# Forgetting attention and a channel mix on one core: the instruction scheduler starts from seeded due times and keeps another pass

## The chip, the cores and the metric

The kernel runs on one core of one Trainium2 chip. The metric is the device time of one execution, in microseconds (us). The core has five engines with queues of their own: PE (TensorE, with PEld for its weight loads), DVE (VectorE), ACT (ScalarE), POOL (GpSimd) and SP (SyncE), which here only issues DMAs.

## What is computed

The reference is an attention with a forgetting bias, and a channel mix on its output. Cut to what matters:

```python
B, H, S, D = 8, 8, 576, 64             # channel mix: d_model 512, d_ff 1024, all float32
scores = (q @ k.T) / sqrt(D)           # per batch and head
cum = cumsum(maximum(s, 0))
scores = where(causal, -1e9, scores + minimum(-(cum[:, None] - cum[None, :]), 0))
attn = exp(scores - scores.max(-1)); attn = attn / (attn.sum(-1) + 1e-9)
x = (attn @ v)                         # heads side by side: (B, S, 512)
x_prev = x shifted by one token
xk = mu_k * x + (1 - mu_k) * x_prev
xr = mu_r * x + (1 - mu_r) * x_prev
out = sigmoid(xr @ w_r) * (maximum(xk @ w_k, 0) ** 2 @ w_v)
```

## The kernel before

**Tiling.** Attention is worked in visits: one visit is a pair of heads of one batch. Batches 0 and 1 are made in an older form (`scores`, line 1226 on, matmuls on lines 1247, 1258 and 1269, PE transposes on line 1649, sums on line 1770); batch 0 is cut into the first three query tiles (A, 64 + 128 + 128 queries) for all four pairs of heads, and then the other two (Z). Batches 2 to 7 are 24 visits of `split_scores`: per head six products, each of two accumulating matmuls on line 1344 (KH with G, then KL with QL, 67 rows), then DVE (line 1356, mask and minimum), ACT (line 1371, exponential), ACT and DVE (lines 1380 and 1387, the reciprocal), ACT (line 1396) and DVE (line 1402), which write the weights as two float16 halves. The DMA turns them, and `sum_values` multiplies them with V for both heads: 32 matmuls in a row on line 1530, into one PSUM tile named pair. `mix_pair` (line 1558 on) mixes neighbouring tokens and splits the result into halves for the channel mix (xkh, xkl on lines 1617 and 1620, by POOL, ACT or DVE).

**The channel mix** takes chunks of 256 tokens, 18 in all. Per chunk there are 96 matmuls of 256 columns with w_k (line 2019), ACT's relu (line 2033) and squares, 24 of 512 columns with w_r (line 2096), ACT's tanh (line 2110), and 48 of 512 columns with w_v (line 2150), whose product DVE takes (line 2161) and a DMA stores. A chunk can be worked as soon as the pairs of heads that cover its tokens are done. The inputs of chunk 0 come straight from the A visits: ACT on line 1947 and DVE on line 1963 mix them. The weights are loaded in a 64-bit form and split into halves by POOL (lines 894, 902), ACT (909, 932, 947) and DVE (914, 921, 938, 960) while the first visits run.

**PSUM.** Scores use two banks named s and two named t, the channel mix two named m, the pair tile the remaining two.

**What sets the order.** Nothing is issued as it is written. Class `Plan` (line 55 on) records each operation as a task: engine, planned length, the tasks that it depends on, and a due time that the program sets by hand (`plan.due`). Helpers `pe`, `act`, `dve`, `pool`, `dma` work out the planned length from columns and a constant (`over` for PE, `extra` for the others); `or_act`, `or_dve`, `or_pool` give a task a second engine that may take it. `Plan.forward` (line 141) is a list scheduler: it runs a model of the engines in time and, whenever one is free, takes the ready task with the least due time. `Plan.backward` (line 295) goes back from the end and returns new due times. `Plan.run` (line 347) repeats forward and backward 60 times and issues the order of the pass whose modelled end was earliest. While PE's first regular scores have not been reached, the scheduler also fills gaps of PE with a matmul of 192 columns on the identity, whose result nobody reads (`one_idle`, its matmul on line 494).

Of the kernel before, what the change touches and what calls it, by code (L numbers as in the profile page):

```python
# [54 lines left out]
class Plan:  # L55
# [283 lines left out]
        return [-x for x in at]  # L339


    PASSES = 60
    engines = ('DVE', 'ACT', 'POOL', 'SP', 'PE')
    LATER = 300.0
    LOCK = 1.0

    def run(self):
        best = None
        due = [t[4] for t in self.tasks]
        for _ in range(self.PASSES):  # L350
            found = self.forward(due)
            if best is None or found[2] < best[2]:
                best = found
            due = self.backward(found[1], found[4])
        order, _, _, emits, on = best
        for n, i in enumerate(order):
            for emit in emits.get(n, ()):
                emit()
            (self.tasks[i] if on[i] == self.tasks[i][0] else self.others[i])[2]()
# [3 lines left out]
def forgetting_attention_then_channel_mix(  # L363
# [16 lines left out]
    nc = tc.nc  # L380

    B, H, D, S = q.shape
    DM, DF = moe_w_k.shape
# [4 lines left out]
    CT = 256  # L388
# [49 lines left out]
    def pool(emit, reads, writes, n, extra, rate=0.8333, quarters=(0, 0)):  # L438
        return at_quarters(plan.add("POOL", n * rate + extra, emit, reads, writes), quarters)
# [895 lines left out]
    def split_scores(passes, F):  # L1335
# [5 lines left out]
        def products(ps, q, m, k0, n):  # L1341
            for x, (G, K, r) in enumerate(passes):
                pe(
                    lambda x=x, G=G, K=K, r=r: nc.tensor.matmul(  # L1344
                        ps.get()[:m, :n],
                        G.get()[:r, q : q + m],
                        K.get()[:r, k0 : k0 + n],
                        start=x == 0,
                        stop=x == 1,
                    ),  # L1350
                    [(G, x) for x in range(2)] + [(K, x) for x in range(2)], [ps], n, m,
                )

        def least(ps, n, mask, i):
# [203 lines left out]
    def mix_pair(b, c, found):  # L1558
# [8 lines left out]
        xm = late_space["xm"]  # L1567
# [13 lines left out]
        for w in range(2):  # L1581
            t = late_space[f"t{w}"]

            def mixed(w=w, t=t):
                nc.vector.scalar_tensor_tensor(
                    out=xm.get()[:, 0:S] if w == 0 else values(), in0=values(),
                    scalar=mu_late.ap[:, w, 0, c : c + 1], in1=t.get()[:, 0:S],
                    op0=ALU.mult, op1=ALU.add,
                )

            dve(
                mixed, [t, (t, "z"), (mu_late, w)] + ([found] if w == 0 else []),
                [found if w else xm], S, extra=100,
            )
        t0 = S * b
        at = t0 % RING
# [3 lines left out]
        for w in range(2):  # L1600
            src = xm if w == 0 else found

            def whole(o, n, w=w):
                return xm.get()[:, o : o + n] if w == 0 else found.get()[:, 448 + o : 448 + o + n]

            for o, n in pieces:
                some = range((t0 + o) // CT, (t0 + o + n - 1) // CT + 1)

                def own(y, o=o, n=n, w=w):
                    p = (t0 + o) % RING  # L1610
                    return row(w, y, c, p, p + n)

                his = [(chunk(w, 0, x), (c, b)) for x in some]
                los = [(chunk(w, 1, x), (c, b)) for x in some]

                def high(engine, own=own, whole=whole, o=o, n=n):
                    engine.tensor_copy(own(0), whole(o, n))  # L1617

                def low(engine, own=own, whole=whole, o=o, n=n):
                    engine.tensor_tensor(out=own(1), in0=whole(o, n), in1=own(0), op=ALU.subtract)  # L1620

                def high_act(own=own, whole=whole, o=o, n=n):
                    nc.scalar.copy(own(0), whole(o, n))

                if w == 0:
                    or_act(
                        pool(lambda f=high: f(nc.gpsimd), [src], his, n, 150),
                        high_act, n, 75,
                    )
                    or_dve(  # L1630
                        pool(lambda f=low: f(nc.gpsimd), [src] + his, los, n, 210, 2.0),
                        lambda f=low: f(nc.vector), n, both=True,
                    )
                else:
                    act(high_act, [src], his, n, 75)
                    dve(lambda f=low: f(nc.vector), [src] + his, los, n)
# [260 lines left out]
    def channel_mix(ch, start, span, after):  # L1897
# [111 lines left out]
        def hidden(fp):  # L2009
# [34 lines left out]
            if ch in range(6):  # L2044
                act(
                    lambda: nc.scalar.activation(kh.get()[:, fs, :], r.get(), AF.Square, scale=2.0**-6),
                    [r], [(kh, fp)], 2 * CT, 75,
                )
                y = act(
                    lambda: nc.scalar.activation(r.get(), r.get(), AF.Square),  # L2050
                    [], [r], 2 * CT, 75,
                )
                or_dve(
                    y,
# [14 lines left out]
            def sq():  # L2069
# [1 line left out]

            act(
                lambda: nc.scalar.activation(kh.get()[:, fs, :], r.get(), AF.Square, scale=2.0**-6),
                [r], [(kh, fp)], 2 * CT, 75,
            )
            dve(
                lambda: nc.vector.scalar_tensor_tensor(
# [12 lines left out]
        def gate(tt):  # L2090
# [32 lines left out]
            def scaled(engine):  # L2123
# [6 lines left out]
                pool(  # L2130
                    lambda: scaled(nc.gpsimd), scale_keys(sc, 3), [(g, 0), (g, DM // 2)], DM, 300
                ),
                DM, 94,
            )
            st["g", tt] = g

# [324 lines left out]
```

## Time and profile before

| | |
|---|---|
| median of 3 runs | 766.78 us (765.98 to 767.72) |
| the profiled execution | 766.97 us, of which its span, first to last instruction, is 765.3 us |
| instructions in the profile | 17015 |
| PE busy | 737.4 us, 96% |
| DVE, ACT, POOL busy | 599.3 us (78%), 590.6 us (77%), 486.9 us (64%) |
| mean granted TensorE clock | 0.984 of full speed |
| read from and written to HBM | 54.09 MB, 12.24 MB |

The profile's busy shares are averages over the whole span. A PE that shows as busy need not be at its peak, since the end of a matmul is modelled and successive matmuls overlap; how far apart two of them start tells more. Of a wait the profile names the engine, line and tile that ended it.

### The profile page before, as it was taken

What the parts mean: (1) busy time and instruction counts of PE and PEld (TensorE: products, weight loads), DVE (VectorE), ACT (ScalarE), POOL (GpSimd) and SP (SyncE); (2) the same over time, 40 slices, a digit from 0 to 9 for tenths busy, and PEclk for the clock granted to TensorE, in tenths of its full rate; (3) what the DMA queues carried; (4) which work ended last, traced back from release to release, by engine and by line L of the source; (5) the groups of instructions that cost most, each with busy time, mean ns of one, the idle gap of its engine ahead of it and who ended that gap; (6) DMA issues with size and microseconds to landing.
All of it is one profiled execution on the core that took longest, in us unless ns stands there. A gap on an engine that the chain in (4) does not pass through costs nothing.

```text
span 765.3 us, 17015 instructions
## 1 busy us (share of the span) xinstructions
PE 737.4 (96%) x5385; PEld 491.7 (64%) x5385; DVE 599.3 (78%) x1825; ACT 590.6 (77%) x1783; POOL 486.9 (64%) x599
## 2 busy tenths in 40 slices
PE   9979999999999889998999999999999999999998
PEld 8847666865675465756575757575757575755664
DVE  7998898878979879998799998888988787613321
ACT  6989999888978888987889888988878887512311
POOL 6697888688358679665977697659864983100000
PEclk9978999999999999999999999999999999999999
DMA  8865744449449958877888789887976766300000
GB/s 250 276 188 187 236 138 125 128 110 192 96 112 173 178 120 179 193 147 148 176 181 172 150 187 180 152 184 155 203 142 133 142 124 95 77 28 15 15 28 28
DMA packets 207338, 109.93 MB, mean 144 GB/s; under 512 B 178000, under 2 KB 183888, under 8 KB 207248
## 3 DMA queue, kind: packets, MB, share of 16 engines
q1 hardware_dynamic: 207248, 108.85, 63.2%
q8 instruction: 42, 0.69, 0.4%
q14 instruction: 48, 0.39, 0.2%
HBM read 54.09 MB, written 12.24 MB: 87 GB/s over the span
## 4 chain that ended last, share of the span: by engine, by line
PE 36%; ACT 17%; DVE 15%; issue 6%; DMA 1%; POOL 1%; SPq 0%; DVEq 0%; ACTq 0%; POOLq 0%
PE m L2150 10%; PE m L2019 6%; PE m L2096 5%; ACT W L1396 4%; DVE W L1402 4%; PE pair L1530 3%; ACT t L1371 3%; ACT s L1371 3%; PE s L1344 2%; DVE t L1356 2%; ACT wd L1575 2%; PE t L2019 2%; PE s L2019 2%; PE t L2150 2%; PE t L1344 2%
## 5 line engine op out<-in xcount | busy, mean ns | idle before, releaser
L2019 PEld LDWEIGHTS <-w_k 128*128 128x128 f16 x1728 | 162.9, 99 | 39.3 <-issue 14.5
L2019 PE MATMUL m<-xkh,w_k 128*128 128x256 f16 x976 | 182.7, 277 | 3.6 <-POOL xkh L1617 2.3
L2150 PE MATMUL m<-w_v,kh 128*128 128x512 f16 x528 | 166.8, 381 | 0.6 <-ACT g L2110 0.6
L2019 PE MATMUL m<-xkl,w_k 128*128 128x256 f16 x488 | 134.8, 277 | 1.6 <-POOL xkl L1620 1.6
L2150 PE MATMUL m<-w_v,kl 128*128 128x512 f16 x264 | 100.5, 382 | 0.0
L1189 POOL TENSOR_TENSOR KH<-raw,KH 64x576 fp32r<-64x576 f32 x64 | 91.5, 1430 | 6.2 <-ACT KH L1178 1.7
L1213 POOL TENSOR_TENSOR QL<-raw,G 64x576 fp32r<-64x576 f32 (+1 forms) x64 | 86.0, 1344 | 12.8 <-ACT G L1202 5.9
L2150 PEld LDWEIGHTS <-kh 128*128 128x128 f16 x592 | 56.4, 98 | 57.3 <-issue 4.9
L2096 PE MATMUL m<-w_r,xrh 128*128 128x512 f16 x264 | 86.7, 382 | 1.0 <-DVE kl L2083 0.4
L1371 ACT ACTIVATE s<-s,nm 128x64 f32<-128x64 f32 (+2 forms) x144 | 61.7, 429 | 20.1 <-DVE nm L1356 12.9
L2124 POOL TENSOR_SCALAR g<-g,scale 128x512 f32<-128x512 f32 x21 | 16.6, 788 | 94.7 <-ACT g L2110 91.2
L1344 PE MATMUL s<-KH,G 128*128 128x64 f32 (+3 forms) x192 | 69.5, 364 | 6.2 <-DVE W L1402 5.5
L1402 DVE SCALAR_TENSOR_TENSOR W<-s,rinv,W 128x64 f16<-128x64 f32 (+1 forms) x144 | 65.5, 455 | 11.4 <-ACT W L1396 10.7
L1396 ACT ACTIVATE W<-s,rinv 128x64 f16<-128x64 f32 (+1 forms) x144 | 65.5, 457 | 7.9 <-DVE rinv L1387 5.4
L1402 DVE SCALAR_TENSOR_TENSOR W<-t,rinv,W 128x320 f16<-128x320 f32 (+1 forms) x96 | 61.7, 645 | 8.8 <-ACT W L1396 8.2
L1344 PE MATMUL s<-KL,QL 67*128 67x64 f32 (+2 forms) x192 | 66.1, 350 | 0.0
L1371 ACT ACTIVATE t<-t,nm 128x320 f32<-128x320 f32 (+1 forms) x96 | 55.5, 578 | 11.0 <-DVE nm L1433 6.8
L1209 POOL CAST G<-raw 128x576 fp32r<-128x576 f32 x48 | 32.9, 685 | 43.7 <-issue 32.6
L1356 DVE CUSTOM_DVE_ANT_0 t<-t,lower 128x320 f32<-128x320 f32 (+1 forms) x96 | 57.0, 597 | 3.5 <-PE t L1344 2.3
L1396 ACT ACTIVATE W<-t,rinv 128x320 f16<-128x320 f32 (+1 forms) x96 | 57.9, 607 | 0.4 <-DVE rinv L1387 0.2
L1530 PE MATMUL pair<-T,V 128*64 128x512 f16 (+6 forms) x768 | 56.1, 300 | 0.1
L2033 ACT ACTIVATE r<-m 128x512 f32<-128x512 f32 x58 | 34.8, 600 | 22.7 <-PE m L2019 19.8
(264 smaller groups left out, 1971.0 us busy)
## 6 DMA issues: line engine op xcount, KB each, us to landing
raw<-in_q SPq DMA_DIRECT2D x112, 144.0 KB
raw<-in_k SPq DMA_DIRECT2D x32, 288.0 KB
vn<-in_v SPq DMA_DIRECT2D x24, 384.0 KB
out<-g SPq DMA_DIRECT2D x35, 256.0 KB
wd<-in_moe_w_v SPq DMA_DIRECT2D x8, 512.0 KB
T<-W SPq DMA_TRANSPOSE x192
V<-in_v SPq DMA_DIRECT2D x8, 320.0 KB
wd<-in_moe_w_k SPq DMA_DIRECT2D x4, 512.0 KB
```

The lines of the kernel that those rows point to most:

```text
L1189: lambda own=own, other=other, K=K: nc.gpsimd.tensor_tensor(out=K.get()[other], in0=k.get()[own], in1=f32(K.get()[own]), op=ALU.subtract),
L1213: lambda x=x, QQ=QQ, QL=QL: nc.gpsimd.tensor_tensor(out=QL.get()[0:64, 0:nq], in0=x.get()[0:64], in1=f32(QQ.get()[0:64]), op=ALU.subtract,),
L1344: lambda x=x, G=G, K=K, r=r: nc.tensor.matmul(ps.get()[:m, :n], G.get()[:r, q : q + m], K.get()[:r, k0 : k0 + n], start=x == 0, stop=x == 1,),
L1356: lambda: nc.vector.tensor_tensor_reduce(out=ps.get()[:, :n], in0=ps.get()[:, :n], in1=mask(), scale=-SCALE, scalar=3.0e38, op0=ALU.add, o ...
L1371: lambda: nc.scalar.activation(ps.get()[:, :n], ps.get()[:, :n], AF.Exp, bias=nm.get()[:, i + o : i + o + 1], scale=-1.0, accum_out=sums.g ...
L1396: lambda: nc.scalar.activation(part(0), ps.get()[:, :n], AF.Copy, scale=rinv.get()[:, i : i + 1]),
L1402: lambda: nc.vector.scalar_tensor_tensor(out=part(1), in0=ps.get()[:, :n], scalar=rinv.get()[:, i : i + 1], in1=part(0), op0=ALU.mult, op1 ...
L1530: nc.tensor.matmul(ps.get()[64 * j : 64 * j + 64, a:e], V.get()[:, block[0], block[1], j], moving(j), start=first, stop=last, tile_positio ...
L2019: lambda u=u, f=f, c=c, n=n, w=w, x=x: nc.tensor.matmul(ps.get()[:, u * CT : (u + 1) * CT], weight["k", c, f // 4].get()[:, w, f % 4 * P : ...
L2033: lambda: nc.scalar.activation(r.get(), ps.get(), AF.Relu, scale=2.0**-26),
L2096: lambda c=c, n=n, x=x, w=w: nc.tensor.matmul(ps.get(), row(1, x, c, place + tt * P, place + tt * P + P), weight["r", c, 0].get()[:, w], s ...
L2150: lambda f=f, i=i, x=x, w=w, ps=ps, columns=columns: nc.tensor.matmul(ps.get()[:, 0:n], x.get()[:, f, ts], weight["v", f, 0].get()[:, w, c ...
```

## The change

Three things are edited, all of them in what the scheduler is given or keeps. The first due times are each shifted by a hash of the task's number and a seed, 1047; with this seed the shift lies between -5000 and +5000 ns. The scheduler makes 51 passes and keeps the last, instead of 60 and the one with the earliest modelled end. And six planned lengths are changed: 17 in place of 7 ns beside the columns of a score matmul of `split_scores`, 131 for 100 ns at DVE's mix of `mix_pair`, a lower cost for POOL's subtraction there (136 ns and 1.94 ns a column for 210 and 2.0), 100 or 97 for 75 ns at ACT's squares, 281 for 94 ns where ACT may scale the gate in POOL's place. No instruction's work changes by it; the order does, and for tasks with two engines, which of them takes each.

```diff
-    PASSES = 60
+    PASSES, SEED = 51, 1047
+    SHIFTS = 500.0, 2000.0, 5000.0, 10000.0
...
+    def shift(self, i):
+
+        x = (self.SEED * 2654435761 + i * 40503 + 12345) & 0xFFFFFFFF
+        x = (x ^ (x >> 15)) * 2246822519 & 0xFFFFFFFF
+        x = (x ^ (x >> 13)) * 3266489917 & 0xFFFFFFFF
+        return self.SHIFTS[self.SEED % 4] * ((x ^ (x >> 16)) / 4294967296.0 - 0.5)
+
     def run(self):
-        best = None
-        due = [t[4] for t in self.tasks]
+        due = [t[4] + self.shift(i) for i, t in enumerate(self.tasks)]
         for _ in range(self.PASSES):
-            found = self.forward(due)
-            if best is None or found[2] < best[2]:
-                best = found
-            due = self.backward(found[1], found[4])
+            best = self.forward(due)
+            due = self.backward(best[1], best[4])
...
-                    [(G, x) for x in range(2)] + [(K, x) for x in range(2)], [ps], n, m,
+                    [(G, x) for x in range(2)] + [(K, x) for x in range(2)], [ps], n, m, over=17,
...
-                [found if w else xm], S, extra=100,
+                [found if w else xm], S, extra=131,
...
-                        pool(lambda f=low: f(nc.gpsimd), [src] + his, los, n, 210, 2.0),
+                        pool(lambda f=low: f(nc.gpsimd), [src] + his, los, n, 136, 1.94),
...
-                DM, 94,
+                DM, 281,
```

Every line number of the changed kernel past line 343 is 5 higher: line 1344 is now 1349, and so on.

Counted over the program, PE has the same matmuls as before but for the identity ones, which go from 85 to 131. Of tasks with two engines, the subtraction on line 1620 goes from 8 on DVE and 28 on POOL to 4 and 32; ACT takes 4 more squares from DVE (line 2050) and DVE 3 more relus from ACT (line 2036); POOL scales 26 gates in place of 24.

**The order at the start.** SP's queue, the first loads of the program. KH and xkh are the keys and queries of the first scores, wd and xrl hold raw weights, V the values, g and vn the bias sums. Before:

```order
L647 DMA g0_115<-in_s_t 128x3x8
L602 DMA vn0_121<-in_s 64x576
L868 DMA wd0_127<-in_moe_w_k 128x1024
L2272 DMA xkh0_129<-in_q 64x320
L2272 DMA xkl0_144<-in_q 64x320
L1123 DMA KH0_155<-in_k 128x320
L1065 DMA V0_164<-in_v 128x384
```

Now:

```order
L652 DMA g0_115<-in_s_t 128x3x8
L607 DMA vn0_121<-in_s 64x576
L873 DMA wd0_127<-in_moe_w_k 128x1024
L873 DMA wd1_138<-in_moe_w_k 128x1024
L1070 DMA V0_163<-in_v 128x384
L2277 DMA xkh0_129<-in_q 64x320
L2277 DMA xkl0_154<-in_q 64x320
L2277 DMA xkh0_129<-in_q 64x320
L1128 DMA KH0_225<-in_k 128x320
```

The second piece of w_k (512 KB), the values (192 KB) and a third load of queries (80 KB) now stand ahead of the first keys. On PE, 72 identity matmuls stand between the bias matmuls (line 1247) and the first scores (line 1258), where 31 stood.

**The order ahead of chunk 0.** DVE's queue just before its first mix for the channel mix (line 1963, now 1968, which writes xp from the A visits' results). Before:

```order
L1332 RECIPROCAL inverses0_332<-inverses0_332 128x2
L1078 TENSOR_REDUCE am1_925<-V0_164 128x1
L780 RECIPROCAL ranges_81<-ranges_81 128x1
L1332 RECIPROCAL inverses0_332<-inverses0_332 128x2
L960 SCALAR_TENSOR_TENSOR w_r_1_00_918<-xrh0_790,unit_79,w_r_1_00_918 128x512
L960 SCALAR_TENSOR_TENSOR w_r_0_00_933<-xrh0_790,unit_79,w_r_0_00_933 128x512
L1678 COPY T2_205<-t0_300 128x128
L1761 TENSOR_TENSOR r160_391<-inverses0_332,r160_391 128x2x2
L960 SCALAR_TENSOR_TENSOR w_r_2_00_928<-xrh0_790,unit_79,w_r_2_00_928 128x512
L1817 TENSOR_TENSOR w_v_7_00_272<-po0_108,w_v_7_00_272 128x320
L1963 SCALAR_TENSOR_TENSOR xp0_346<-w_v_4_00_262,mu_g0_93,xp0_346 128x256
```

Now:

```order
L1289 ISA W00_322,nm0_323<-s1_167,lower_98 128x288
L1289 ISA nm0_323 128x1
L1020 TENSOR_SCALAR unit_79<-unit_79 128x1 x2
L1289 ISA W00_322,nm0_323<-s0_160,lower_98,nm0_323 128x288
L1289 ISA nm0_323 128x1
L1018 RECIPROCAL unit_79<-most_r_77 128x1
L733 TENSOR_SCALAR ranges_81<-ranges_81 128x1
L965 SCALAR_TENSOR_TENSOR w_r_3_00_879<-xrh0_730,unit_79,w_r_3_00_879 128x512
L1968 SCALAR_TENSOR_TENSOR xp0_349<-w_v_5_00_289,mu_g0_93,xp0_349 128x256
```

Sixteen of DVE's operations moved from ahead of the mix to behind it, among them two of three splits of w_r (line 960), three mask passes of the Z visits (line 1284) and one of the A visits' four results (line 1817). On ACT sixteen moved past its first mix (line 1947) too. On PE 48 transposes and 14 of the Z visits' score matmuls stand ahead of the first channel-mix matmul (line 2019), where it was 55 and 18.

**The order around the pair sum before chunk 4.** PE's queue; s0 to t1 are the score banks, m1 a bank of the channel mix. Before:

```order
L2150 MATMUL m1_319<-w_v_7_00_1750,kh0_1158 128x512
L1344 MATMUL s1_171<-KH1_625,G0_599 128x192
L1344 MATMUL s1_171<-KL0_649,QL0_131 128x192
L1344 MATMUL t1_291<-KH2_627,G1_639 128x320
L1344 MATMUL t1_291<-KL1_669,QL1_140 128x320
L1344 MATMUL s0_166<-KH1_625,G0_599 128x448
L1344 MATMUL s0_166<-KL0_649,QL0_131 128x448
L1344 MATMUL t0_300<-KH2_627,G1_639 128x512
L1344 MATMUL t0_300<-KL1_669,QL1_140 128x512
L1344 MATMUL s1_171<-KH2_627,G1_639 128x64
L1530 LDWEIGHTS V1_2535
L1530 MATMUL pair_3097<-T0_2345,V1_2535 64x512
```

Now:

```order
L2155 LDWEIGHTS kh0_1147
L2155 MATMUL m1_252<-w_v_7_00_1738,kh0_1147 128x512
L2155 LDWEIGHTS kl0_1177
L2155 MATMUL m1_252<-w_v_7_00_1738,kl0_1177 128x512
L2155 LDWEIGHTS kh0_1147
L2155 MATMUL m1_252<-w_v_7_00_1738,kh0_1147 128x512
L1349 MATMUL t0_377<-KH2_769,G1_587 128x512
L1349 MATMUL t0_377<-KL1_754,QL1_141 128x512
L1535 LDWEIGHTS V1_2585
L1535 MATMUL pair_3068<-T0_2385,V1_2585 64x512
```

Nine score matmuls stood in a row there, with no matmul of the channel mix among them; now two stand together, with ten or more channel-mix matmuls between them and the pair of scores ahead. Over the program, runs of six or more such score matmuls go from six (the longest 9 and 8) to four (each of 6).

## Rows read from the trace of the kernel before

**Rows 1.** The page: the span, and part 1, busy time by engine.

```profile
span 765.3 us, 17015 instructions
PE 737.4 (96%) x5385; PEld 491.7 (64%) x5385; DVE 599.3 (78%) x1825; ACT 590.6 (77%) x1783; POOL 486.9 (64%) x599
```

**Rows 2.** Busy us by window: PE, PEld, DVE, ACT, POOL; granted clock; DMA share; GB/s.

```profile
0.00:12.00 12.00, 10.09 (x84) 9.43 (x85) 9.17 (x21) 5.55 (x13) 8.21 (x38) 1.00 0.74 194
...
39.30:58.80 19.50, 14.31 (x72) 9.07 (x70) 18.79 (x74) 16.77 (x51) 18.10 (x23) 0.69 0.65 190
...
78.40:165.00 86.60, 85.31 (x707) 61.15 (x708) 74.34 (x242) 80.75 (x253) 67.64 (x84) 1.00 0.49 142
165.00:256.00 91.00, 88.53 (x610) 55.46 (x607) 78.73 (x237) 78.14 (x239) 62.93 (x81) 1.00 0.71 151
256.00:272.00 16.00, 11.41 (x81) 7.24 (x79) 13.38 (x49) 13.09 (x49) 7.45 (x10) 0.89 0.88 181
...
344.00:357.20 13.20, 10.89 (x92) 7.99 (x90) 11.31 (x32) 10.02 (x32) 6.70 (x7) 0.87 1.05 197
357.20:600.00 242.80, 240.08 (x1766) 157.24 (x1764) 212.56 (x654) 207.87 (x642) 182.06 (x209) 1.00 0.81 165
...
662.00:765.30 103.30, 99.29 (x662) 62.82 (x660) 27.21 (x41) 24.69 (x39) 8.12 (x10) 1.00 0.06 21
```

**Rows 3.** The page's part 5: a channel-mix matmul, with busy us, mean ns.

```profile
L2019 PE MATMUL m<-xkh,w_k 128*128 128x256 f16 x976 | 182.7, 277 | 3.6 <-POOL xkh L1617 2.3
```

**Rows 4.** Timeline of PE, 655 to 660 us: start, us, line, tile.

```profile
654.96 0.27 PE L2019 MATMUL m<-xkl,w_k 128*128 128x256 f16 x1
...
659.55 0.27 PE L2019 MATMUL m<-xkl,w_k 128*128 128x256 f16 x1
```

**Rows 5.** Timeline of PE, the start and the first channel-mix matmul.

```profile
5.70 2.73 PE L494 MATMUL po<-ident 128*128 128x192 bf16 x31
8.27 0.78 PE L1258 MATMUL s<-KH,xkh 128*128 128x192 f32 x4
...
58.15 0.61 PE L1269 MATMUL s<-KH,G 128*128 128x288 f32 x1 [1.82 <-DVE nm L1284]
58.55 0.44 PE L1269 MATMUL s<-KL,QL 67*128 67x288 f32 x1
58.80 0.65 PE L2019 MATMUL m<-xkh,w_k 128*128 128x256 f16 x2
```

**Rows 6.** DVE's groups up to 56.6 us, by form: busy us, mean ns of one.

```profile
L960 DVE SCALAR_TENSOR_TENSOR w_r<-xrh,unit,w_r 128x512 f16<-128x512 f32 x3 | 2.8, 924 | 0.2 <-ACT w_r L947 0.2
...
L1817 DVE TENSOR_TENSOR w_v<-po,w_v 128x320 f32<-128x320 f32 x4 | 1.9, 474 | 0.0
...
L1284 DVE CUSTOM_DVE_ANT_0 W<-s,lower 128x448 f32<-128x448 f32 x2 | 1.2, 615 | 0.0
...
L1284 DVE CUSTOM_DVE_ANT_0 W<-s,lower,nm 128x288 f32<-128x288 f32 x2 | 1.0, 504 | 0.0
...
L1078 DVE TENSOR_REDUCE am<-V 128x1 bf16<-128x640 f32 x1 | 0.8, 804 | 0.0
...
L1761 DVE TENSOR_TENSOR r<-inverses,r 128x4 f16<-128x4 f32 x1 | 0.7, 731 | 0.0
```

**Rows 7.** Timeline of PE around the pair sum before chunk 4.

```profile
256.84 0.31 PE L1344 MATMUL t<-KL,QL 67*128 67x320 f32 x1
259.75 0.47 PE L1344 MATMUL s<-KH,G 128*128 128x448 f32 x1 [2.59 <-DVE W L1402]
...
261.86 3.80 PE L1530 MATMUL pair<-T,V 128*64 128x512 f16 x32
265.59 0.30 PE L1344 MATMUL s<-KL,QL 67*128 67x64 f32 x1
```

**Rows 8.** Timeline of PE: a pair sum and the waits before chunk 6, and chunk 15's.

```profile
345.86 2.27 PE L1530 MATMUL pair<-T,V 128*64 128x512 f16 x32
348.06 0.30 PE L1344 MATMUL s<-KH,G 128*128 128x64 f32 x1
...
351.27 0.38 PE L2019 MATMUL m<-xkh,w_k 128*128 128x256 f16 x2 [1.33 <-POOL xkh L1617]
352.62 0.27 PE L2019 MATMUL m<-xkl,w_k 128*128 128x256 f16 x1 [0.98 <-POOL xkl L1620]
...
667.42 0.27 PE L2019 MATMUL t<-xkh,w_k 128*128 128x256 f16 x1 [0.39 <-POOL xkh L1617]
```

**Rows 9.** Timeline of PE: the last pair sum of the attention.

```profile
662.04 2.27 PE L1530 MATMUL pair<-T,V 128*64 128x512 f16 x32
```

More of the change, by code (lines that the diff above doesn't have):

```diff
@@ L2046, in hidden @@
                     lambda: nc.scalar.activation(kh.get()[:, fs, :], r.get(), AF.Square, scale=2.0**-6),
-                    [r], [(kh, fp)], 2 * CT, 75,
+                    [r], [(kh, fp)], 2 * CT, 100,
                 )
@@ L2050, in hidden @@
                     lambda: nc.scalar.activation(r.get(), r.get(), AF.Square),
-                    [], [r], 2 * CT, 75,
+                    [], [r], 2 * CT, 100,
                 )
@@ L2073, in hidden @@
                 lambda: nc.scalar.activation(kh.get()[:, fs, :], r.get(), AF.Square, scale=2.0**-6),
-                [r], [(kh, fp)], 2 * CT, 75,
+                [r], [(kh, fp)], 2 * CT, 97,
             )
```

## The prediction

> **What bounds the kernel now.** First the page: of a span of 765.3 us PE is busy for 737.4 [rows 1], so PE looks like the bound, with only 27.9 us idle. Then how far apart matmuls start. In the quiet stretch near 655 us there are 42 matmuls of 256 columns from 654.96 to 659.55 us [rows 4], 109 ns each, while the page gives one of them 277 ns [rows 3]. So a busy share holds time in which PE does not run at its rate, and a wait shorter than about 170 ns never shows as idle. The Trainium skill says as much (Perfetto Trace Analysis, Identifying the Most-Contended Engine): matmul busy share is no good measure of how close PE is to its peak. By the busy share no order could win more than 27.9 us; by the starts there is more that an order decides, and the sum below goes by starts and waits.
>
> PE's matmuls are the same in number and size, but for the identity ones, so the time is PE's fixed work plus what PE loses to waits, to idle matmuls and to the clock. The view by windows shows where [rows 2]. From 39.3 to 58.8 us PE is busy for 14.31 of 19.5 us while DVE is for 18.79: there DVE is the bound, and the granted clock is 0.69. From 78.4 to 165 us PE is busy for 85.31 of 86.6. From 165 to 600 us it loses little except in two short windows, 256 to 272 us (11.41 of 16.0, clock 0.89) and 344 to 357.2 us (10.89 of 13.2, clock 0.87). The last 103.3 us are PE alone. In that tail and in the long middle PE never waits for long, so what is won or lost earlier is carried to the end.
>
> **The change, part by part.** The planned lengths and the shift cost nothing on the chip; only the order that they lead to does.
>
> *The start.* 31 identity matmuls fill 5.70 to 8.27 us [rows 5], 83 ns each. 41 more before the first scores are 3.4 us, and all 46 are 3.8 us. They are issued, not skipped, so PE's first score comes no earlier than 8.27 + 3.4 = 11.7 us. This matters to the end only if what follows waits for it.
>
> *Chunk 0.* What follows is bound by DVE. The first channel-mix matmul starts at 58.80 us, after a wait for DVE of 1.82 us just before it [rows 5]. Sixteen DVE operations now stand behind chunk 0's first mix: two splits of w_r at 924 ns, a mask pass of 615 ns and two of about 504 ns, a reduction of 804, a small product of 731 and one of 474 [rows 6], together 5.5 us, and eight or so small ones that I put at 150 to 280 ns each by their like, 1.4 us. That is 6.9 us less in the queue that ended last. DVE was idle for 2.8 of its first 12 us already [rows 2], and the changed queue puts weight work into the time in which the scores are late, so the late start need not be lost again. At worst it is lost whole: the first channel-mix matmul then comes 6.9 - 3.4 = 3.5 us earlier; at best 6.9 us. PE has a little less done by then, 7 transposes and 4 score matmuls, at 109 to 300 ns about 1.6 us. The net is 1.9 to 5.3 us. The moved work has to be done afterwards, but PE then has chunk 0 to work on. **I take -3.0 us**; the ends kept for the range are -6.9 and, if DVE's shorter queue buys nothing, +3.8.
>
> *The pair sum before chunk 4.* Before, nine score matmuls stand together with nothing of the channel mix among them. The score banks are freed by a chain over DVE and ACT, so PE stops for 2.59 us at 259.75 [rows 7], the clock falls to half (1.2 of 2.4 GHz), and the 32 matmuls of the pair sum take 3.73 us (261.86 to 265.59) [rows 7], where the same sum at full clock takes 2.20 (345.86 to 348.06) [rows 8]. 2.59 + 1.53 and half a microsecond of smaller waits are 4.6 us. Now the pairs of scores there have ten or more matmuls of 512 columns between them, over 2 us of work at 218 ns (twice the 109). **I take -3.5 us**, since part of a wait usually turns up at the next step; bounds 0 and -4.6.
>
> *Before chunks 6 and 15.* PE waits for POOL to split the last pair's result, 1.33 and 0.98 us before chunk 6, and 0.39 before chunk 15 [rows 8]. The number of matmuls between that pair sum and the one that waits goes from 16 to 23 before chunk 6 (5 of them of the channel mix, 0.5 us, the rest scores; 1.1 us in all) and from 36 to 81 before chunk 15. **I take -1.5 us**; bounds 0 and -3.9, the latter with the half clock after that wait gone too (344 to 357.2 us at 0.87 is 3.4 us at half, worth 1.7). Before chunk 4 the distance stays (17 and 18 matmuls), so that wait should remain.
>
> *New waits.* An order made anew has some of its own, and I can't see them without times. The nearest rows: the calm stretch from 357.2 to 600 us loses 2.7 us of 242.8, and 165 to 256 us loses 2.5 of 91 [rows 2]. **I take +2.4 us**; bounds 0 and +7, the latter if a stretch like 256 to 272 us (4.6 us idle) and one like 344 to 357.2 (2.3) come up elsewhere.
>
> *Engines.* POOL takes four more of the subtractions and two more gate scalings; it is busy for 64% [rows 1]. Four squares go to ACT and three relus to DVE. These lie beside PE's work, and I cost them at nothing; if POOL's cover goes, the keys and queries that it splits come late and the scores wait.
>
> The sum: -3.0 - 3.5 - 1.5 + 2.4 = -5.6 us. The profiled execution took 766.97 us (span 765.3 and 1.7 around it), within 0.2 us of the median of 766.78, so I use it as it is: **761.4 us**. About 0.2%, 1.5 us, can be told from no change.
>
> **Rivals.**
> *The late start is a plain loss (slower).* Place: the first 12 us. PE's work is fixed, so 46 idle matmuls more are 3.8 us more unless the wait for DVE before chunk 0 shrinks; and if that wait is set by a chain (scores, mask, exponential, transposes, sums) and not by the length of DVE's queue, all of it starts 3.4 us later. With the other terms trading even, 766.97 + 3.8 = 770.8 us. It decides at the first channel-mix matmul: 58.8 us or later is this rival. For it: the wait at 58.15 us follows a chain [rows 5]. Against it: DVE is busy for 18.79 of 19.5 us [rows 2].
>
> *Attention keeps its pace and the tail is longer (slower).* After the last pair sum, at 662.04 us [rows 9], 676 matmuls are left where it was 628; the 48 more have 256 columns, 5.2 us at 109 ns. If DVE and ACT set the pace of the attention, that pair sum moves only by the work they no longer have ahead of it, some 4.0 us on DVE by its rows, and the time is 766.97 + 5.2 - 4.0 = 768.2 us, or 772.2 if even that buys nothing. My forecast asks for a last pair sum at about 651 us. For it: DVE is busy for 212.56 of 242.8 us from 357.2 to 600 [rows 2]. Against it: that is 88%, and PE is at 99% there, so PE and not DVE paces it.
>
> *Waits are only traded (no change).* The two bad places go, others come, 767 us. For it: the terms at two places of 25 us are all that I can name in 435 us. Against it: the runs of scores standing together are shorter, six to nine before, six at most now.
>
> **How the numbers follow.** Forecast 761.4 us, chance 0.56. Traded waits, 0.18, spread evenly around 767, of which most lies within 0.2%. Late start 0.14, the longer tail 0.12. Faster by over 0.2% (below 765.2): the forecast and a little of the traded case, 0.60. Within 0.2%: 0.15. Slower: 0.25, both slow rivals bar the part of the second that lies just inside. Range: below, the forecast with chunk 0 and the two places at their full price and no more than 2.4 us of new waits, 766.97 - 6.9 - 4.6 - 3.9 + 2.4 = 754.0; above, the late start at 770.8, which leaves the worst of the tail out. So 754.0 to 770.8.
>
> **What would show it.** Right: the first channel-mix matmul at 52 to 56 us; no wait of over 1 us and no half clock between 250 and 265 us; a wait before chunk 4 that stays, and one before chunk 6 about 1 us shorter; the last pair sum at 649 to 653 us and a tail of 108.5 us after it. Wrong: a first channel-mix matmul at 58.8 us or later, a last pair sum past 657 us, or a new stretch with PE below 85% busy between 165 and 600 us. The order says nothing of how full the queues of POOL and DMA are when the scores are asked for, so the likeliest thing to break it is keys that come late.

## The result, and the profile after

The changed kernel takes 757.93 us (median of 4 runs, 757.77 to 758.79), the one before 766.38 beside it (765.98 to 767.72, 4 runs): a ratio of 0.9889, 95% interval 0.9872 to 0.9906, or 8.5 us less. The profiled execution took 757.77 us with a span of 756.1, 9.2 less than before. All line numbers of the changed kernel are 5 higher than before from line 344 on.

The page and the windows of the changed kernel (columns as in [rows 2]):

```profile
span 756.1 us, 17136 instructions
...
PE 735.0 (97%) x5431; PEld 494.0 (65%) x5431; DVE 592.5 (78%) x1824; ACT 585.8 (77%) x1780; POOL 492.5 (65%) x603
```

```profile
39.30:58.80 19.50, 17.10 (x130) 12.25 (x130) 18.20 (x79) 18.37 (x63) 17.89 (x23) 0.92 0.65 200
165.00:256.00 91.00, 86.58 (x581) 54.12 (x579) 77.74 (x241) 79.38 (x250) 59.57 (x74) 1.00 0.71 153
256.00:272.00 16.00, 14.12 (x125) 10.53 (x122) 15.06 (x54) 14.78 (x50) 11.50 (x17) 1.00 1.00 175
344.00:357.20 13.20, 11.91 (x97) 9.49 (x96) 11.85 (x37) 11.55 (x37) 6.74 (x11) 1.00 0.93 171
357.20:600.00 242.80, 239.63 (x1759) 155.81 (x1759) 212.70 (x656) 209.44 (x652) 190.82 (x211) 1.00 0.85 167
652.80:756.10 103.30, 100.16 (x659) 64.15 (x656) 28.67 (x43) 25.32 (x41) 7.72 (x10) 1.00 0.06 21
```

PE is idle for 6.8 us less (21.1 for 27.9) and busy for 2.4 us less, though 46 more identity matmuls (3.8 us at 83 ns) count as busy. So part of the gain is idle time that went or was filled, and part is time in which PE was busy below its rate. In the three bad windows PE is busy for longer (17.10 for 14.31 us, 14.12 for 11.41, 11.91 for 10.89), in two calm ones for a little less (86.58 for 88.53, 239.63 for 240.08). These windows are cut by time, so the two kernels do not do the same work in them.

The timeline of PE in the changed kernel, at the places that the prediction named:

```profile
5.80 7.12 PE L499 MATMUL po<-ident 128*128 128x192 bf16 x72
12.75 0.72 PE L1263 MATMUL s<-KH,xkh 128*128 128x192 f32 x3
...
54.05 0.88 PE L1654 MATMUL t<-ident,W 128*128 128x128 f32 x4 [1.31 <-ACT w_v L1816]
...
55.18 0.39 PE L2024 MATMUL m<-xkh,w_k 128*128 128x256 f16 x2
...
256.88 2.27 PE L1535 MATMUL pair<-T,V 128*64 128x512 f16 x32
...
262.57 0.27 PE L2024 MATMUL m<-xkh,w_k 128*128 128x256 f16 x1 [0.86 <-POOL xkh L1622]
263.46 0.27 PE L2024 MATMUL m<-xkl,w_k 128*128 128x256 f16 x1 [0.62 <-POOL xkl L1625]
...
343.54 0.38 PE L2024 MATMUL m<-xkh,w_k 128*128 128x256 f16 x2 [0.46 <-POOL xkh L1622]
344.89 0.27 PE L2024 MATMUL m<-xkl,w_k 128*128 128x256 f16 x1 [0.97 <-POOL xkl L1625]
...
648.48 2.27 PE L1535 MATMUL pair<-T,V 128*64 128x512 f16 x32
```

The first regular scores come 4.5 us later (12.75 for 8.27), the first channel-mix matmul 3.6 us earlier (55.18 for 58.80) [rows 5]. The pair sum before chunk 4 has no long wait ahead of it and runs at full clock, 2.27 us for 3.80 [rows 7]. The waits for POOL before chunk 6 are 0.9 us shorter together [rows 8]. Those before chunk 4 stay; they were, in PE's timeline of before:

```profile
268.71 0.27 PE L2019 MATMUL m<-xkh,w_k 128*128 128x256 f16 x1 [0.98 <-POOL xkh L1617]
269.61 0.27 PE L2019 MATMUL m<-xkl,w_k 128*128 128x256 f16 x1 [0.62 <-POOL xkl L1620]
```

The last pair sum comes 13.6 us earlier [rows 9].

**Where the 9 us come from.** Since PE's work is the same, the two traces can be laid over each other by work: each matmul counts as the lower quartile of the start-to-start times of its kind in the trace of before, the identity matmuls count nothing, and the table gives by how much a kernel reaches the same amount of work earlier than the one before (us; negative: later). The totals agree within 1.1 of 658 us, and no row can be trusted further than that. Each column is one execution of its kernel: by the medians of all runs the kernels end 0.3 to 2.3 us less ahead than the last row has it ("lengths" 0.6 us more), so 1 or 2 us between two columns say little, while the steps within a column show the places. The other columns are the experiments below.

```
work  before  after  start   rest  middle  to320  to313  b-mid  lengths  s1051
   5    14.1   -5.8   -5.4   -0.4    -0.2   -5.6   -4.9   -5.8     -0.5   -1.1
  35    65.1    3.4    4.5   -0.6    -0.2    4.3    5.4    4.6      3.7    1.4
  80   115.4    3.8    4.0   -0.4    -0.1    4.1    4.8    3.9      1.1    2.1
 140   178.5    3.8    1.5   -1.2    -0.1    3.4    4.2    3.2      0.3   -0.3
 200   247.5    2.0    1.9   -3.2    -3.2    1.7    2.4    2.5     -3.7   -1.8
 215   271.5    6.6    2.1    1.4     1.9    6.8    7.5    2.8     -1.2    0.2
 230   289.4    8.2    2.0    3.3     3.6    8.4    9.2    4.7     -1.8   -5.0
 275   340.3    7.5    2.2    2.8     3.0    7.7    8.5    3.9     -2.2   -3.0
 290   360.9    9.7    1.9    5.0     5.2   10.0   10.7    6.2      1.5   -1.2
 335   412.6    9.7    2.2    5.0     2.9    8.2   11.1    6.1      2.3   -0.5
 485   577.3    5.4    2.0    1.0     2.2    7.9   10.6    1.9     -0.5   -7.0
 575   678.6    9.4    1.6    5.0     2.2    7.3   10.2    5.7      2.0   -4.4
 650   753.7    9.4    1.6    5.0     2.2    7.3   10.2    5.8      2.2   -4.4
```

The changed kernel wins 3.8 us up to 80 us of work, loses 1.8 up to 200, wins 6.2 around the pair sum before chunk 4 (200 to 230), 2.2 around chunk 6 (275 to 290), loses 4.3 from 335 to 485 and gets 4.0 back from 485 to 575.

### The profile page after: what moved, and what is told of

Its sections match the earlier page's. It is cut to its first block, busy times and chain, and to the rows that moved or that the text cites. A ratio compares the mean times of both kernels' runs of the same rounds, so it can differ in the third digit from the quotient of the medians.

```text
span 756.1 us, 17136 instructions
## 1 busy us (share of the span) xinstructions
PE 735.0 (97%) x5431; PEld 494.0 (65%) x5431; DVE 592.5 (78%) x1824; ACT 585.8 (77%) x1780; POOL 492.5 (65%) x603
## 4 chain that ended last, share of the span: by engine, by line
PE 69%; ACT 13%; DVE 11%; issue 4%; POOL 1%; DMA 1%; SPq 0%; ACTq 0%; DVEq 0%; POOLq 0%
PE m L2155 17%; PE m L2024 14%; PE m L2101 7%; PE pair L1535 4%; PE s L1349 4%; PE t L1349 3%; PE t L1654 3%; PE po L1775 2%; PE s L1274 2%; ACT W L1401 2%; DVE W L1407 2%; ACT t L1376 2%; PE po L499 2%; PE t L2024 2%; PE s L2024 2%
## 5 line engine op out<-in xcount | busy, mean ns | idle before, releaser
L2024 PEld LDWEIGHTS <-w_k 128*128 128x128 f16 x1728 | 163.2, 98 | 38.4 <-issue 10.2
L1376 ACT ACTIVATE s<-s,nm 128x64 f32<-128x64 f32 (+1 forms) x144 | 61.7, 428 | 22.4 <-DVE nm L1361 14.5
L1349 PE MATMUL s<-KH,G 128*128 128x64 f32 (+3 forms) x192 | 67.3, 354 | 6.0 <-DVE W L1407 5.4
L1349 PE MATMUL s<-KL,QL 67*128 67x64 f32 (+2 forms) x192 | 61.6, 333 | 0.0
L2166 DVE TENSOR_TENSOR g<-g,m 128x512 f32<-128x512 f32 x33 | 22.5, 683 | 39.2 <-PE m L2155 38.9
```

The costliest lines, as they stand in the source:

```text
L1349: lambda x=x, G=G, K=K, r=r: nc.tensor.matmul(ps.get()[:m, :n], G.get()[:r, q : q + m], K.get()[:r, k0 : k0 + n], start=x == 0, stop=x == 1,),
L1376: lambda: nc.scalar.activation(ps.get()[:, :n], ps.get()[:, :n], AF.Exp, bias=nm.get()[:, i + o : i + o + 1], scale=-1.0, accum_out=sums.g ...
L2024: lambda u=u, f=f, c=c, n=n, w=w, x=x: nc.tensor.matmul(ps.get()[:, u * CT : (u + 1) * CT], weight["k", c, f // 4].get()[:, w, f % 4 * P : ...
```

## The experiments

My theory was that these gains belong to places and add up. The rivals: they hang together, so that a lead won at one place is taken back at the next; or the lengths, the seed or the clock explains them.

### Which edit, and which seed

Only the planned lengths (no shift, 60 passes):

```diff
-                    [(G, x) for x in range(2)] + [(K, x) for x in range(2)], [ps], n, m,
+                    [(G, x) for x in range(2)] + [(K, x) for x in range(2)], [ps], n, m, over=17,
...
```

> Only the six planned lengths are changed; no shift, 60 passes, the pass with the earliest modelled end. In its order the nine scores in a row before chunk 4 are gone too (four at most stand there), 13 DVE operations fewer stand ahead of chunk 0's first mix, and 692 matmuls are left after the last pair sum (628 before, 676 with the whole change). If the time follows from these places (my theory): about -3 at chunk 0, -4 at the pair sum, and later waits that I can't see, so 759 to 763 us. Rival, the picked seed carries the gain and the lengths do nothing: 765 to 768 us.

Only the shift and the 51st pass:

```diff
-    PASSES = 60
+    PASSES, SEED = 51, 1047
...
```

> Only the shift by seed 1047 and the 51st pass; the six planned lengths as before. Its order has 18 idle matmuls before the first scores (49 before, 90 with the whole change), 15 DVE operations fewer ahead of chunk 0's first mix than before, no scores in a row before chunk 4, and 695 matmuls after the last pair sum. By these places: first channel-mix matmul at 53 to 56 us, no half clock near 260 us, 757 to 762 us. Rival, the seed was picked for these lengths and means nothing with others: 764 to 770 us, from waits elsewhere.

The whole change with the neighbouring seed:

```diff
-    PASSES, SEED = 51, 1047
+    PASSES, SEED = 51, 1051
```

> The whole change, but with the neighbouring seed 1051, which has the same scale of shift (10000). Only 8 DVE operations fewer stand ahead of chunk 0's first mix than before, 18 idle matmuls before the first scores, no scores in a row before chunk 4, 685 matmuls after the last pair sum. If the gain comes from the pair sum's place and the lengths, which a seed hardly touches: 758 to 762 us, with a first channel-mix matmul 1 to 2 us later than with seed 1047. Rival, the gain is that of one lucky seed: 764 us or more.

Measured: lengths alone 763.70 us, ratio 0.9966 (0.9953 to 0.9978); seed alone 766.87, 0.9997 (0.9989 to 1.0006); seed 1051 773.14, 1.0080 (1.0066 to 1.0094). The lengths alone give a third of the gain, 0.7 us short of what I had forecast. The seed alone gives nothing, and its neighbour costs 6.6 us, so the second and third of my forecasts were wrong. All three orders have what I had named, no nine scores in a row before chunk 4 and a channel mix that starts at 54.3 to 56.6 us, and they lose it elsewhere. (Ahead of the first scores the seed alone and seed 1051 have 46 and 57 identity matmuls, not 18 as I had it.) With the seed alone PE waits 1.60 us for ACT before chunk 4 and works at half clock from 266.77 to 273.60 us by the record of the granted clock, against what I had expected there (PE's timeline):

```profile
267.56 0.37 PE L2024 MATMUL m<-xkh,w_k 128*128 128x256 f16 x1 [1.60 <-ACT xkh L1628]
```

Seed 1051 loses 5.2 us between 215 and 230 us of work and 6.5 between 335 and 485; PE's timeline at the first of the two:

```profile
283.91 0.38 PE L2101 MATMUL m<-w_r,xrl 128*128 128x512 f16 x1
288.39 0.61 PE L1349 MATMUL t<-KH,G 128*128 128x320 f32 x1 [4.10 <-DVE W L1407]
```

A score has its turn in PE's order before DVE has freed its bank, and PE stops for 4.10 us: the same kind of wait as the one of before at 259.75 us [rows 7], at another pair, and longer. Two good features in an order say little about the other 700 us.

### The order in pieces

Here an order written out in a table takes the place of the scheduler; every task is the one of before, and the cut is put where PE has a given amount of work behind it.

```diff
     def run(self):
-        best = None
...
+        raw = zlib.decompress(base64.b85decode(ORDER))
+        for v in struct.unpack(f"<{len(raw) // 2}h", raw):
+            if v < 0:
+                self.idle()
+            else:
+                (self.others if v & 1 else self.tasks)[v >> 1][-1 if v & 1 else 2]()
```

The start alone ("start" in the table):

```diff
+ORDER: changed order to 80 us of work, then the order before
```

> Every task in the changed kernel's order until PE has about 80 us of work behind it, and the order before from there. Places add up (my theory): the start is worth what its first channel-mix matmul shows in the changed kernel, 58.8 - 55.2 = 3.6 us, and with the small waits up to 80 us about 4; the pair sum before chunk 4 again waits about 2.6 us and runs at half the clock. So 766.4 - 3.8 = 762.6 us. Rival, the lead is taken back at the next place where PE waits for the attention's chain (coupled waits): 766 us or a little under, with longer waits between 256 and 272 us than before. Rival, the late start is a loss that other places pay for: 768 us or more.

All but the start ("rest"):

```diff
+ORDER: order before to 80 us of work, then the changed order
```

> The order before until PE has about 80 us of work behind it, and the changed order from there: chunk 0 and its start are left as they were. Places add up: 766.4 less the rest of the gain, 8.5 - 3.8 = 4.7 us, so about 761.5, first channel-mix matmul at 58.8 us, no half clock between 256 and 272 us. Coupled waits: the later order is made for an early start and meets waits of its own without it, 764 to 766 us.

The middle alone ("middle"):

```diff
+ORDER: order before to 150 us of work, changed order to 320, then the order before
```

> The changed order only for the stretch in which PE goes from 150 to 320 us of its work (the pair sum before chunk 4, and chunk 6), the order before on both sides. Places add up: over this stretch the changed kernel gains 6.5 us on the one before, so 766.4 - 6.5 = 760 us, and it should beat the start alone. Coupled waits: the gain needs the lead from the start, and 763 to 766 us come out.

The first half ("to320"):

```diff
+ORDER: changed order to 320 us of work, then the order before
```

> The changed order until PE has 320 us of its work behind it, the order before from there. In the changed kernel the lead over the one before is about 10 us at that point, and falls to 5.4 by 485 us through new waits at 407, 482 and 512 us before it comes back. Places add up: 766.4 - 10 = 756.5 us, level with the changed kernel or up to 1.5 us under it. Coupled waits: the later waits are a price of the lead itself, since the attention can't keep it up, and the order before shows them too: 760 to 762 us.

Measured: start 765.21 us, ratio 0.9981 (0.9969 to 0.9992); rest 762.65, 0.9948 (0.9936 to 0.9960); middle 765.71, 1.0001 (0.9989 to 1.0013; three of its eleven runs took 767.9 us or more); first half 760.39, 0.9930 (0.9914 to 0.9946). Every one gains less than I forecast, so by their times alone the rival of coupled waits is ahead. The table says something else. Between the cuts each piece does what it does in the changed kernel: the start is 4.0 us ahead at 80, "rest" and "middle" win 6.5 and 6.8 us from 200 to 230, and away from the cuts no lead loses more than 0.9 us in all to the order before. In three of the four what is missing goes just behind a cut: 2.5 us in "start" (80 to 140), 2.3 in "middle" and 1.8 in "to320" (290 to 335). In the last, PE waits for DVE, and DVE had stood still for a load (timelines of PE and DVE in "to320"):

```profile
391.73 0.27 PE L2019 MATMUL m<-xkh,w_k 128*128 128x256 f16 x1 [1.10 <-DVE kl L2083]
```

```profile
388.88 0.82 DVE L1078 TENSOR_REDUCE am<-vn 128x1 bf16<-128x640 f32 x1 [2.33 <-DMA vn<-in_v]
```

The load's issue stood behind the cut, DVE had its reduction early, and everything in DVE's queue waited with it; PE's wait is 1.10 of the 1.8 us. So I cut where nothing of DVE and ACT is on the wrong side ("to313"):

```diff
+ORDER: changed order to 313 us of work, then the order before
```

> The changed order until PE has 313 us of its work behind it, then the order before; at this cut no operation of DVE or ACT stands on the wrong side, unlike at 320. If the 2 us lost behind the cut at 320 were the cut's own (one split of the channel mix came late there): the lead of 10 us is kept and the time is 757 to 758.5 us, level with the changed kernel. If the attention can't keep up with the lead: a loss of 2 us or more between 315 and 345 us of work again, 760 us.

Measured: 758.55 us, ratio 0.9897 (0.9882 to 0.9911). The lead is kept, 10.7 us at 290 and 10.2 at the end of this execution, and the time is that of the changed kernel. So the loss at 320 was the cut's own (by a late load, as its trace has it, where I had named a late split). It also says what the last half of the changed order is worth: nothing. The changed kernel gives up 4.3 us of its lead and takes 4.0 back; the order before does neither.

The other loss, up to 200 us of work, is of another kind. "Rest", "middle" and both scheduler orders in the table have it, 1.5 to 4 us, and after it a gain at 215. I put the order before into that stretch alone ("b-mid"):

```diff
+ORDER: changed order to 153 us of work, order before to 205, then the changed order
```

> The changed order but for the stretch from 153 to 205 us of PE's work, which has the order before. In that stretch every order without the nine scores in a row loses 1 to 3.5 us to waits, and the order before loses nothing there but 4.6 us right behind it. If the two belong together (scores that are asked for early wait for their keys and banks; asked for late, they stand in a row): the loss ahead goes and the wait at the pair sum comes back, 759 to 762 us. If they are independent: 755.5 to 756.5 us, faster than the changed kernel by 1.5 to 2.

Measured: 761.30 us, ratio 0.9929 (0.9917 to 0.9941). From 140 to 200 the loss shrinks from 1.8 to 0.7 us, and from 200 to 230 only 2.2 us are won where it was 6.2, since the long wait is back (PE's timeline):

```profile
250.84 0.22 PE L1344 MATMUL s<-KL,QL 67*64 67x64 f32 x1
253.93 0.53 PE L1344 MATMUL s<-KH,G 128*128 128x192 f32 x1 [2.87 <-DVE W L1402]
```

The two belong together: scores asked for early wait a little, several times, for DVE to free their banks (six waits, 3.2 us together, from 165 to 275 us in the changed kernel); asked for late they stand in a row and wait once, for long. The pair sum's place is worth its 6.2 us less the 1.8 ahead of it by the table, 4.4; by the times of this run and of the changed kernel it is 3.4 us.

### What the start hangs on

The idle matmuls of the changed order cut from 72 to 31 ahead of its first scores:

```diff
-L499 MATMUL po<-ident 128x192 x72
+L499 MATMUL po<-ident 128x192 x31
```

> The changed kernel's order with 41 of the idle matmuls before its first scores left out; nothing else is moved. If these idle matmuls hold up the start (its first scores come 4.5 us later than before: 3.4 us of it the idle matmuls): first scores 3 us or so earlier, first channel-mix matmul up to 3 us earlier, 755 to 757 us. Rival, the loads and DVE's queue set the start and the idle matmuls only fill the time: first scores, first channel-mix matmul and end as in the changed kernel, 757.5 to 758.5 us. Third, they keep PE's clock up: a half clock in the first 15 us and a time above 758.5 us.

Measured: 759.85 us, ratio 0.9904 (0.9888 to 0.9920). PE's timeline:

```profile
5.32 2.73 PE L494 MATMUL po<-ident 128*128 128x192 bf16 x31
11.47 1.27 PE L1258 MATMUL s<-KH,xkh 128*128 128x192 f32 x4 [3.42 <-DMA KH<-in_k]
...
263.47 0.27 PE L2019 MATMUL m<-xkh,w_k 128*128 128x256 f16 x1 [0.87 <-POOL xkh L1617]
264.37 0.37 PE L2019 MATMUL m<-xkl,w_k 128*128 128x256 f16 x1 [0.62 <-POOL xkl L1620]
```

The scores wait for a load: without the filling PE stops for 3.42 us, starts only 1.3 us earlier, at half clock (11.6 to 15.0 us by the record of the granted clock), and the first channel-mix matmul comes at 55.88, not earlier. That is the third case: the idle matmuls cost 1.3 us at most and keep the clock up. That the end comes 1.9 us later is not clear of noise: its six runs spread from 756.35 to 761.10, and the two intervals overlap. In the profiled execution (760.54 us) chunk 4's first matmuls ran at half clock from 264.19 to 267.60 us, after the same two waits for POOL that the changed kernel has at full clock (0.86 and 0.62 us).

The order before, with 90 idle matmuls where PE waits between 40 and 58 us:

```diff
+L494 MATMUL po<-ident 128x192 (90 in all, at 13 places of PE's order)
```

> The kernel before with 90 identity matmuls added at 13 places of PE's order between 40 and 58 us, where PE waits for DVE; nothing moves. Rival (the start's gain is the clock that the fuller PE keeps up, not DVE's shorter queue): full clock through this stretch, the first 17 us of chunk 0 no longer at half rate, 3 to 4 us gained, 763 us. My theory: DVE's queue still ends where it did, first channel-mix matmul at 58.5 to 59.5 us; what the kernel before lost behind it to the half clock (56.8 to 63.6 us) comes back at most, some 1 to 2.5 us: 764 to 766 us.

Measured: 767.25 us, ratio 1.0006 (0.9997 to 1.0015). The window and PE's timeline:

```profile
39.30:58.80 19.50, 16.93 (x153) 12.98 (x153) 18.87 (x74) 16.67 (x49) 18.28 (x23) 1.00 0.62 189
```

```profile
57.78 1.73 PE L494 MATMUL po<-ident 128*128 128x192 bf16 x19
59.29 0.38 PE L1269 MATMUL s<-KH,G 128*128 128x288 f32 x1
...
59.64 0.39 PE L2019 MATMUL m<-xkh,w_k 128*128 128x256 f16 x2
```

The clock is whole (1.00 for 0.69 [rows 2]) and nothing is won. The last 19 fillers ran up to the score that they stand before and may have cost it up to 1 us; the 3 to 4 us of the rival are not there in any case. The Trainium skill (TensorE: Matmul & The Clock Gate, HAM oscillation — how this bites in real kernels) reckons half of the throttled time as lost: by it, an estimate, the 12.1 us at half clock that 0.69 of 19.5 us means would be worth 6 us. The run gives at most the 1 us that the last fillers may have cost: PE is not what the stretch waits for, it is idle for 5.2 of these 19.5 us [rows 2].

Five of DVE's operations moved behind the first operation of chunk 0's first mix, nothing else:

```diff
-L960 w_r, L960 w_r, L960 w_r, L1078 am, one pass: in DVE's order ahead of L1963 xp
+the same five, right behind the first L1963 xp
```

> The kernel before with five of DVE's operations (the three splits of w_r on line 960, a reduction and a small pass; by the profile of before about 4.0 us together) put right behind chunk 0's last mix; PE, ACT and POOL keep their order. If DVE's queue alone sets the first channel-mix matmul (my theory): it starts at 55 to 56 us instead of 58.8, and the time falls by 2.5 to 4 us, 762.5 to 764. Rival, a chain sets it: 58 us or later and 765.5 to 767. In between, if chunk 0's matmuls with w_r now wait for their split: 55 to 56 us, but 765 us and a wait for the w_r tile some 15 us later.

Measured: 770.43 us, ratio 1.0045 (1.0033 to 1.0058): slower. Timelines of DVE, ACT and PE in this run:

```profile
56.46 0.49 DVE L1963 SCALAR_TENSOR_TENSOR xp<-w_v,mu_g,xp 128x256 f32<-128x256 f32 x1 [1.27 <-ACT xp L1947]
56.85 0.82 DVE L1078 TENSOR_REDUCE am<-V 128x1 bf16<-128x640 f32 x1
57.58 2.33 DVE L960 SCALAR_TENSOR_TENSOR w_r<-xrh,unit,w_r 128x512 f16<-128x512 f32 x3
59.83 0.48 DVE L1817 TENSOR_TENSOR w_v<-po,w_v 128x320 f32<-128x320 f32 x1
60.23 0.47 DVE L1963 SCALAR_TENSOR_TENSOR xp<-w_v,mu_g,xp 128x256 f32<-128x256 f32 x1
```

```profile
55.38 0.97 ACT L1947 ACTIVATE xp<-w_v,mu_g 128x256 f32<-128x256 f32 x2
...
60.74 0.65 ACT L1987 CAST xkh<-xp 128x256 f16<-128x256 f32 x2 [3.82 <-DVE xp L1963]
```

```profile
61.30 0.61 PE L1269 MATMUL s<-KH,G 128*128 128x288 f32 x1 [3.93 <-DVE nm L1284]
...
61.94 0.65 PE L2019 MATMUL m<-xkh,w_k 128*128 128x256 f16 x2
```

On DVE the first mix is two operations, and the five landed between them, not behind both as I had meant. So ACT's cast (line 1987) waits 3.82 us for the second, the score that PE reaches first waits 3.93 us for DVE where it waited 1.82 [rows 5], and the first channel-mix matmul comes at 61.94 us. The time of this run therefore does not decide on my theory of the start; the start of the mix does. With 4 us taken out of its way DVE stands idle and waits for ACT's half of the mix, which is ready at 56.35 us, and starts at 56.46. Before it started at 56.56, but the first scores of this run came 1.0 us later (9.31 for 8.27): counted from them, 4.0 us less in the queue bring the mix 1.1 us. The trace of before agrees: ACT's half was ready at 55.32 us, and DVE came to the mix 1.2 us later. So DVE's queue ended last, but by 1.2 us only, and my theory, that it alone sets the start, is wrong.

ACT's half needs the scaled mixing factors mu_g, which POOL makes from maxima over the weights. The timeline of all engines, first of before, then of the changed kernel:

```profile
46.33 0.36 POOL L750 TENSOR_TENSOR shares<-mu,most_r 128x4 f32<-128x4 f32 x2
...
46.72 0.17 DVE L756 TENSOR_REDUCE tops<-shares 128x1 bf16<-128x8 f32 x1 [0.31 <-POOL shares L750]
...
52.78 1.62 POOL L814 TENSOR_SCALAR mu_g<-shares,ranges,scale 128x8 f32<-128x8 f32 x2
...
54.35 0.97 ACT L1947 ACTIVATE xp<-w_v,mu_g 128x256 f32<-128x256 f32 x2
...
56.56 1.00 DVE L1963 SCALAR_TENSOR_TENSOR xp<-w_v,mu_g,xp 128x256 f32<-128x256 f32 x2
```

```profile
41.99 0.35 POOL L755 TENSOR_TENSOR shares<-mu,most_r 128x4 f32<-128x4 f32 x2
...
47.63 0.35 POOL L819 TENSOR_SCALAR mu_g<-shares,ranges,scale 128x8 f32<-128x8 f32 x1
...
48.62 0.99 ACT L1952 ACTIVATE xp<-w_v,mu_g 128x256 f32<-128x256 f32 x2
...
49.91 1.00 DVE L1968 SCALAR_TENSOR_TENSOR xp<-w_v,mu_g,xp 128x256 f32<-128x256 f32 x2
...
51.33 0.36 ACT L1992 CAST xkh<-xp 128x256 f16<-128x256 f32 x1
```

The chain runs 4.3 us earlier at shares, 5.2 at mu_g, 5.7 at ACT's half and 6.6 at DVE's. With the lengths alone it is seen as a wait; ACT's timeline in that run:

```profile
49.40 0.99 ACT L1947 ACTIVATE xp<-w_v,mu_g 128x256 f32<-128x256 f32 x2 [0.89 <-POOL mu_g L814]
```

There ACT stands ready, and mu_g is what it waits for. In the traces of before, of the run above and of the changed kernel the profile shows no wait of ACT there: in the changed kernel mu_g is done 0.6 us before ACT comes to the mix (47.98 and 48.62), and ACT is busy with other work until then. So the first mix hangs on a chain from the shares over their maxima (DVE, transposed by PE on line 738) to mu_g and ACT's half, and at each link on the queue of the engine that has it. That fits the gain at the mix, but which link brings it was not tried.

Nor is the mix all: in the changed kernel both parts of xkh are done at 51.69 us, and PE comes to its first channel-mix matmul only at 55.18, behind four transposes that had waited 1.31 us for ACT (54.05 in its timeline above). Of the mix's 6.6 us, 3.6 are left there. What in the order brings the 3.8 us of the start is therefore open.

## Why the prediction was right, and where not

The forecast was 761.4 us with a range from 754.0 to 770.8; 757.93 came. The direction and the places were right, the gain too small by 3.5 us. Step by step, on the scale of the spans (-9.2 where the sum had -5.6):

- **Chunk 0, -3.0.** Measured -3.6 at the first channel-mix matmul (52 to 56 us forecast, 55.18 came) and -3.8 at 80 us of work. The size is right by luck, and the reason was wrong. "6.9 us less in the queue that ended last" took a busy engine for the bound: that queue ended last by 1.2 us only, and 4.0 us out of it brought the first mix 1.1 us. Behind it stand ACT's queue and a chain through mu_g; the mix came 6.6 us earlier, and PE used 3.6 of them. The late-start rival did name a chain, though another one (scores to sums), and concluded that all of it starts 3.4 us later; the links have their own places in the order, and those of mu_g's chain moved forward.
- **The late start.** Lost 5.8 us at 5 us of work, regained by 35. I put it down to the idle matmuls; a load sets it but for 1.3 us at most, and they fill the wait.
- **The pair sum before chunk 4, -3.5.** The nine scores, the wait and the half clock are gone as said. Measured -6.2 from 200 to 230 us of work, with a price of 1.8 ahead of it: -4.4 net. The gross gain is above my bound of 4.6, which held only the wait, the clock and half a microsecond. The run that gives this stretch the order before puts the net at 3.4 us.
- **Chunks 6 and 15, -1.5.** Chunk 6: -2.2 (275 to 290), of which 0.9 is the two waits and the rest mostly the half clock that I had kept for the bound. The wait before chunk 4 stayed, as said.
- **New waits, +2.4.** 1.8 ahead of the pair sum, 0.7 from 230 to 275 and 0.4 net from 290 to the end: +2.9, of the forecast size. The sum is -3.8 + 1.8 - 6.2 + 0.7 - 2.2 + 0.4 = -9.3 us.
- **The longer tail.** The last pair sum came at 648.5 us (649 to 653 forecast), the rest after it took 107.6 (108.5). With the order before from 313 us on it comes at 652.4, and the time is within a microsecond: where the last pair sum stands says how the work is dealt out between middle and tail, not how long it takes.
- **Waits only traded.** Wrong for this order; for the seed alone it is what happened (766.87 us). The chance of 0.25 for slower was not too high: the neighbouring seed lands there, with the same places in its order, for which I would have forecast (and did, 758 to 762 us) a gain too. That the order of seed 1047 has no such loss elsewhere is luck as far as the forecast goes.

No piece or mixture beat the changed kernel; the best, with the changed order up to 313 us of work, is level with it.

## What to carry to other kernels

Lay two traces of the same work over each other by work done, not by time: the lead shows at once where an order wins and what it pays for it just ahead, and a cut that costs something of its own can be told from a gain that is lost. Before a full queue is called the bound, find the last operation that the waiting one needs and follow its inputs back; an engine that is busy for 96% of a stretch may be doing work that nobody waits for yet. A seed is worth what it measures for exactly this program: the same edit with the neighbouring seed came out 6.6 us slower than before, so measure again after every other change.

## What I had not expected of the hardware

Half clock can cost next to nothing: 24 us of the execution before were at half rate by the record of the granted clock; the fillers gave back the 17 us of them between 43 and 64 us, and the time stayed at 1.0006 (0.9997 to 1.0015) of before, so that they had cost about 1 us at most, which is what the fillers may have taken themselves. Where PE runs without a wait it shows in full: the pair sum before chunk 4 took 3.80 us at half and 2.27 at full clock. And like waits need not lead to it: after waits of 0.87 and 0.62 us for POOL the clock fell at chunk 4's first matmuls in the run with fewer identity matmuls, and after 0.86 and 0.62 us it stayed whole in the changed kernel.

The start of one order varies more than its middle: the first regular scores came at 12.75, 12.74, 12.10, 11.83 and 11.78 us in five kernels that share the changed order up to there, one execution each, and the lead at 5 us of work differed by 0.9 us among them.
